# Keeping gate and up weights of the last two chunks' MLP in one set of buffers

## The chip, the cores and the metric

The kernel runs on one core of a Trainium2 chip. The metric is device time in microseconds (us) of one launch; lower is better.

## The reference

One transformer block is computed on a sequence of 2048 rows of width 640, in bfloat16. A vector `c` gives six modulation vectors.

```
mod = silu(c) @ w_mod                       # six vectors of 640: sa, ca, ga, sb, cb, gb
h = layernorm(x) * (1 + ca) + sa
q, k, v = h @ wqkv                          # 32 heads of 20
o = softmax(q @ k.T * 20**-0.5) @ v
x = x + ga * (o @ wo)
h = layernorm(x) * (1 + cb) + sb
x = x + gb * (((h @ w_gate) * (h @ w_up)) @ w_down)     # inner width 1536
```

## The kernel before

**Tiling.** The query rows are cut into five chunks (`CHUNKS`): three of 512 rows and two of 256. A chunk's attention is done in eight items of four heads each. Scores are made by TensorE (`L1491`) with keys on the partitions and queries along the free axis. Two ways lead from scores to exponentials. Most go to ScalarE, 1024 columns at a time (`L1529`, tile `PP`). The rest, in quads of four units of 512 columns, go to VectorE: it evicts each unit as int16 (`L1553`, tile `DB`), takes two terms out of the four with bit operations (`L1585` and `L1593`, tiles `DSS`), and multiplies one of them by the int16 bits read as bfloat16 (`L1590`, or in four pieces on GpSimd, `L1645`). TensorE multiplies both kinds by the values (`L2158`), summing an item in one PSUM bank. At the end of an item VectorE transposes that bank (`L1723`), takes the reciprocal of the sums (`L1727`), the product is made by GpSimd (`L1729`; for the last item by VectorE), VectorE transposes back (`L1737`, tile `OcT`), and four to five small DMAs copy the rows into place in `Ocp` (`L1750`).

**The suffix of a chunk.** When a chunk's eight items are done, `suffix(ci)` adds the work behind attention: the output projection (`wo` with `Ocp`, `L950` or `L946`), the residual and second layer norm, the transpose of the normed rows (`L1902`), gate and up blocks, the down projection (`wd` with `hprod`) and the stores (`L2048`). The gate and up weights are 12 blocks of 128 inner columns; each block is two loads of 160 KB (`L1956`), one for the gate and one for the up half. A block of a 256-row chunk is ten matmul steps into one PSUM bank; then the gate half is copied to `gsb` (`L1978` on VectorE, `L1979` on ScalarE) and multiplied with the up half into `hprod` (`L1985` on VectorE). For all chunks but the last, this work is laid between the score groups of the next chunk's attention, so chunk 3's MLP runs during chunk 4's attention; chunk 4's own suffix is the tail of the kernel. In chunk 3, TensorE's 128-wide operands are split into four 32-column matmuls ("quarters", `L950`), in chunk 4 they are whole (`L946`).

**Weight buffers.** Three buffers `stg` hold streamed blocks in rotation; a load waits until the block three before it has been used. The last chunk has, besides, ten resident buffers `stx` that are loaded ahead, without rotation. Five of them (`stx_121` to `stx_125`) lie in the storage of the queries `QT` of earlier chunks and may be loaded when those chunks' scores are done; five (`stx_130` to `stx_134`) lie in the storage of chunk 2's suffix and may be loaded when that suffix is finished. The number is computed from the space that is left:

```
nsx = min(11, (q_dead - t_size) // (2 * KD * 128 * 2))
...
while len(stx) < 11 and C.off + 2 * KD * 128 * 2 <= C.end:
    stx.append(C.alloc("stx", [128, 2, KD, 128], BF16))
nsq, nsx = nsx, len(stx)
```

**What sets the order.** The program is written down by a list scheduler (`Sched`) that runs while the kernel is built. Each piece of work is a task with an engine, an estimated duration, dependencies, a priority and a gate (a number of score groups that must have been reached). The result is a fixed order per engine, joined by semaphores. All loads and stores after the start are issued by one queue, SP's, in its order: a load that waits for its buffer holds up what stands behind it. The constants of the scheduler (`STAGE` and others) are the same in both kernels, but as durations and dependencies of tasks change, the order that it writes may change from there on.

Of the kernel before, what the change touches and what calls it, by code (L numbers as in the profile page):

```python
# [329 lines left out]
def emit_program(nc, sched, nsem_dma=56):  # L330
# [97 lines left out]
    with nc.Block() as block:  # L428
# [20 lines left out]
        def _(e):  # L449
# [4 lines left out]
CHUNKS = ((0, 512), (512, 512), (1024, 512), (1536, 256), (1792, 256))  # L454
# [3 lines left out]
         (1, 2, 1, 2, 2, 1, 1, 2),  # L458
         (0, 2, 1, 1, 3, 0, 3, 2))
HALF = (0, 0, 0, 0, 0)  # L460
D_LEAD = 0.451
NB0, NSS = 3, 3
XB0, XSS = 0, 0
# [130 lines left out]
def build_kernel(nc, A_x, A_wqkv, A_wo, B_x, B_w_gate, B_w_up, B_w_down, c, w_mod, out):  # L594
    S, D, H, DH = A_x.shape[1], A_x.shape[2], 32, 20
    KD = D // 128
# [3 lines left out]
    NSET = 8  # L600
    VW = DH + 1
    NC = len(CHUNKS)
# [127 lines left out]
    h2T = R2.alloc("h2T", [128, KD, 512], BF16)  # L730
# [22 lines left out]
    t_size = 0  # L753
    if NALT:
# [3 lines left out]
        t_size = T.off - qt_off  # L758
    nsx = min(11, (q_dead - t_size) // (2 * KD * 128 * 2))
    stx = [at("stx", [128, 2, KD, 128], BF16, qt_off + t_size + i * 2 * KD * 128 * 2) for i in range(nsx)]  # L760
    if NALT:
# [6 lines left out]
        nsq, nsx = nsx, len(stx)  # L768
# [44 lines left out]
    def act(dur, f, deps=(), prio=3.0, **k):  # L813
        return sc.add(Task("act", dur, f, deps, prio=prio, **k))

    def dma(eng, nbytes, f, deps=(), prio=3.0, **k):
        dur = k.pop("dur", 400.0)
        return sc.add(Task(eng, dur, f, deps, prio=prio, nbytes=nbytes, **k))
# [144 lines left out]
    def X(n):  # L963
        return max(n / 2.4 + 3.0, 60.0)
# [356 lines left out]
    for it, (ci, j) in enumerate(items):  # L1321
# [6 lines left out]
        for kg in range(nkg):  # L1328
            for s in range(4):
                u = Unit()  # L1330
# [18 lines left out]
    for it in range(len(items)):  # L1349
        na = len(item_info[it]["acts"])  # L1350
        dus = [u for q in item_info[it]["quads"] for u in q]
        for x, u in enumerate(dus):
            due.append(max(18.0, a0 + na * (x / len(dus) - STAGE.get(it, {}).get("DL", D_LEAD))))
        a0 += na
# [10 lines left out]
    NG = len(glist)  # L1365
# [10 lines left out]
    for tc in range(4):  # L1376
# [6 lines left out]
        if tc == 0:  # L1383
# [3 lines left out]
            x0_done = []  # L1387
        if tc == 3:
            x0_done = [t for l in t_xn.values() for t in l]
# [106 lines left out]
    score_q = []  # L1496
# [50 lines left out]
    for qi, (it, us) in enumerate(dquads):  # L1547
        st_ = d_state[qi]
        for x, u in enumerate(us):
            cell = {}  # L1550
# [219 lines left out]
    bset_done = [{}, {}]  # L1770
    sStg = [Slots(list(range(NSTG)), "stg") for _ in range(2)]

    def half_blocks(ci, nb, o_, t_h, h2T, hprod, hp, u_last, gate, pr, gb, bd):
        n = 256
        g_use = sfx_done.setdefault("gsb", {})
        for fc in range(nb):
# [38 lines left out]
                    sStg[w_].done(wbuf[w_]["i"], task)  # L1815
            r.last.on_start = off

    def suffix(ci):
        alt = NALT and ci >= NC - 2
        bd = bset_done[1 if NALT and ci == NC - 2 else 0]  # L1820
        hprod, h2T, xck, xn2 = set_r if not alt else set_t if ci == NC - 2 else set_c
# [6 lines left out]
        tail = ci == NC - 1  # L1828
        qf = full if tail and TAILX else quarters
        t0 = q0 // 128  # L1830
        gb = int(gstart[ci + 1]) if not tail else 0
# [18 lines left out]
        for tl in range(ntl):  # L1850
            ev = []
            for hf in range(2):
                mms = []
                for k in range(KD):
                    f = qf(320, lambda k=k, tl=tl: Ocp[:, slot, k, tl * 128:(tl + 1) * 128],
                                 lambda k=k, hf=hf: wo_sb[:, k, 320 * hf:320 * hf + 320], k == 0, k == KD - 1 and not tail)
# [8 lines left out]
                def after(r, tl=tl, hf=hf, fx=fx, pq=pq):  # L1865
                    f = lambda e: e.tensor_tensor(xck[:, tl, 320 * hf:320 * hf + 320], ps[:, r.b["b"], 0:320],
                                                  xck[:, tl, 320 * hf:320 * hf + 320], ALU.add)
                    if tail and OP_EARLY:
                        fs_ = fx if isinstance(fx, list) else [fx]
                        r.last = sc.add(Task("pe", C320, [lambda e, g_=g_: g_(e, r.b["b"]) for g_ in fs_], [r.last, oc_ready[ci][-1]],  # L1870
                                             ctr="pex", prio=pq - 1000, name=f"op{ci}.{tl}", mode=r.last.mode))
                    return [dve(ps_cost(320), f, [r.last, d_xc], prio=EV_OP if tail else 1)]
# [23 lines left out]
        tr_l = []  # L1896
        nhalf_ = HALF[ci] if n == 512 else 0

# [36 lines left out]
        hp = []  # L1935
# [9 lines left out]
            half_blocks(ci, nhalf_, o_, t_h2[5 * hf_:5 * hf_ + 5], h2T, hprod, hp, u_last, gate, pr, gb, bd)  # L1945
        g_use = sfx_done.setdefault("gsb", {})
        for fc in range(nhalf_, FT):
            use_x = tail and fc < nsx
            wbuf, dm = [], []
            for w_, wv in enumerate((wgv, wuv)):  # L1950
                cell = {}
                if use_x:
                    cell["t"] = stx[fc][:, w_, :, :]

                def f(e, wv=wv, fc=fc, cell=cell):
                    return e.dma_start(cell["t"], wv[:, :, fc * 128:(fc + 1) * 128])  # L1956
                t = dma("sp", 2 * 128 * KD * 128 * 2, f, sfx_done["qdead"] if use_x and fc < nsq else first if use_x else kp_use if ci == 0 else [], prio=16 + ci + .01 * fc,
                        gate=int(gstart[NC] - 40) if tail and not use_x else 0 if tail else max(0, gb + (STG_G0 if ci == 0 else STG_G)))
                if not use_x:
                    t.acq = [(sStg[w_], "s", 1)]  # L1960

                    def on0(task, cell=cell, w_=w_):
                        cell["i"] = task.slots["s"]
                        cell["t"] = stg[cell["i"]][:, w_, :, :]
                    t.on_start = on0
                wbuf.append(cell)
                dm.append(t)
            gs = fc % 2
            if n <= 256 and GU_ONE:
                mms = []  # L1970
                for w_ in range(2):
                    for k in range(KD):
                        f = qf(n, lambda k=k, cell=wbuf[w_]: cell["t"][:, k, :], lambda k=k: h2T[:, k, 0:n],
                                     k == 0, k == KD - 1, w_ * n)
                        mms.append((X(n), f))

                def after(r, gs=gs, fc=fc):
                    f = lambda e: e.tensor_copy(gsb[:, gs, 0:n], ps[:, r.b["b"], 0:n])  # L1978
                    fa = lambda e: e.copy(gsb[:, gs, 0:n], ps[:, r.b["b"], 0:n])  # L1979
                    ds = [r.last] + ([g_use[gs]] if gs in g_use else []) + sc_use  # L1980
                    if tail:
                        eg = act(n / 1.2 + 60, fa, ds, prio=1e6)
                    else:
                        eg = evac(n, ps_cost(n), f, fa, ds)
                    f = lambda e: e.tensor_tensor(hprod[:, fc, 0:n], ps[:, r.b["b"], n:2 * n], gsb[:, gs, 0:n], ALU.mult)  # L1985
                    return [eg, dve(ps_cost(n), f, [r.last, eg] + (first if alt else bd.get("hp", []) + proj_early + kv_last), prio=1)]
                r = Round(mms, t_h2 + dm + sfx_done.get("ul", []), after, pr(), gate=gate(2 * KD * n), name=f"u{ci}.{fc}")
                g_use[gs] = r.evac[1]
                hp.append(r.evac[1])
                u_last.append(r.last)  # L1990
                if not use_x:
                    def off(task, wbuf=wbuf):
                        for w_ in range(2):
                            sStg[w_].done(wbuf[w_]["i"], task)
                    r.last.on_start = off
                continue
            for w_ in range(2):
                mms = []
                for k in range(KD):
                    f = qf(n, lambda k=k, cell=wbuf[w_]: cell["t"][:, k, :], lambda k=k: h2T[:, k, 0:n],  # L2000
                                 k == 0, k == KD - 1)
                    mms.append((X(n), f))
                if w_ == 0:
                    def after(r, gs=gs):
                        f = lambda e: e.tensor_copy(gsb[:, gs, 0:n], ps[:, r.b["b"], 0:n])  # L2005
                        ds = [r.last] + ([g_use[gs]] if gs in g_use else []) + sc_use
                        fa = lambda e: e.copy(gsb[:, gs, 0:n], ps[:, r.b["b"], 0:n])
                        if tail:
                            return [act(n / 1.2 + 60, fa, ds, prio=1e6)]
                        return [evac(n, ps_cost(n), f, fa, ds)]  # L2010
                    r = Round(mms, t_h2 + [dm[0]] + sfx_done.get("ul", []), after, pr(), gate=gate(KD * n),
                              name=f"g{ci}.{fc}")
                    eg = r.evac[0]
                else:
                    def after(r, gs=gs, fc=fc, eg=eg):
                        f = lambda e: e.tensor_tensor(hprod[:, fc, 0:n], ps[:, r.b["b"], 0:n], gsb[:, gs, 0:n], ALU.mult)
                        return [dve(ps_cost(n), f, [r.last, eg] + (first if alt else bd.get("hp", []) + proj_early + kv_last), prio=1)]
                    r = Round(mms, t_h2 + [dm[1]] + sfx_done.get("ul", []), after, pr(), gate=gate(KD * n), name=f"u{ci}.{fc}")
                    g_use[gs] = r.evac[0]
                    hp.append(r.evac[0])  # L2020
                    u_last.append(r.last)
                if not use_x:
                    r.last.on_start = lambda task, w_=w_, cell=wbuf[w_]: sStg[w_].done(cell["i"], task)
        dn_last = []
        outs = []
        for tl in range(ntl):
# [4 lines left out]
            for (c_, w) in cuts:  # L2031
                mms = []
                for fc in range(FT):
                    f = qf(w, lambda fc=fc, tl=tl: hprod[:, fc, tl * 128:(tl + 1) * 128],
                           lambda fc=fc, c_=c_, w=w: wd_sb[:, fc, c_:c_ + w], fc == 0, fc == FT - 1)
# [6 lines left out]
                if tail and TAILX:  # L2042
# [6 lines left out]
                            prio=1))  # L2049
# [7 lines left out]
    for it in range(len(items)):  # L2057
        ci, j = items[it]
# [542 lines left out]
```

## Time and profile before

| | us |
|---|---|
| median of 3 runs | 813.44 (812.14 to 813.45) |
| the profiled execution | 813.98 |
| its span, first to last instruction | 812.1 |
| ScalarE's exponentials (`L1529`), 808 of them | 744.1 |
| TensorE's scores (`L1491`) | 316.2 |
| output projection of the last chunk starts | 778.61 |

Times within the trace count from the start of the span. A row of the timeline gives start, length, engine, line, operation, what is written and read, and how many instructions were merged; a bracket gives the idle time of that engine before it and what ended it. `PE` is TensorE, `PEld` its weight loads, `DVE` VectorE, `ACT` ScalarE, `POOL` GpSimd, and `SPq` the SP queue issuing a DMA. The granted clock of TensorE is a share of its full speed; its mean over the span is 0.998.

### The profile page before, as it was taken

The page shows a single profiled execution, that of the slowest core. Times are in us where ns is not written, and L with a number is a line of the kernel's source. Part 1 is how long each engine was busy: PE and PEld are TensorE (multiplying, and loading weights), DVE is VectorE, ACT ScalarE, POOL GpSimd, SP SyncE. Part 2 cuts the span into 40 slices and gives each one's busy share as a digit, 9 for nine tenths or more (in the row PEclk, how much of TensorE's full clock was granted, in tenths as well). Part 3 has the DMA queues.
Part 4 walks back from the last instruction along what each step waited for, and adds up shares of the span by engine and source line. Part 5 has one row for each costly group of instructions (what it writes and reads, how often), then busy time and mean ns, then how long its engine had stood idle before and what let it go on. Part 6 is the DMA issues. An engine that isn't in the chain of part 4 may idle for free.

```text
span 812.1 us, 29384 instructions
## 1 busy us (share of the span) xinstructions
PE 793.5 (98%) x12609; PEld 303.1 (37%) x12609; DVE 695.3 (86%) x1272; ACT 764.0 (94%) x853; POOL 324.2 (40%) x334
## 2 busy tenths in 40 slices
PE   8999999999999999999999999999999999999998
PEld 4433333222232232233333333332244334454567
DVE  7979987899989999989998999999698775788773
ACT  7889999999999999999999999999999999999722
POOL 3304266545453452264533434314565250534400
PEclk9999999999999999999999999999999999999999
DMA  9634211114330144100301221004001236005520
GB/s 311 204 85 105 71 46 38 49 38 122 89 67 25 36 126 112 34 6 25 102 5 30 51 57 31 15 19 91 13 6 37 48 79 150 17 21 131 116 70 17
DMA packets 116448, 54.74 MB, mean 67 GB/s; under 512 B 83915, under 2 KB 116319, under 8 KB 116319
## 3 DMA queue, kind: packets, MB, share of 16 engines
q1 hardware_dynamic: 115391, 51.72, 24.5%
q8 instruction: 100, 1.64, 0.8%
q10 hardware_dynamic: 928, 1.15, 0.4%
q14 instruction: 29, 0.24, 0.1%
HBM read 41.85 MB, written 8.41 MB: 62 GB/s over the span
## 4 chain that ended last, share of the span: by engine, by line
PE 64%; ACT 27%; DVE 3%; issue 3%; DMA 2%; SPq 1%; ACTq 0%
ACT PP L1529 27%; PE ps_all L1491 21%; PE ps_all L950 20%; PE ps_all L2158 15%; PE ps_all L946 3%; PE ps_all L1210 2%; DVE DB L1553 1%; PE ps_all L2525 1%; PE ps_all L1146 1%; DMA wm<-in_w_mod_dram 1%; SPq L1750 1%; PE ps_all L1902 1%; PE ps_all L1107 1%; DMA stg<-in_B_w_up_dram 0%; DVE DSS L1585 0%
## 5 line engine op out<-in xcount | busy, mean ns | idle before, releaser
L1529 ACT ACTIVATE PP<-ps_all 128x1024 bf16<-128x1024 f32 x808 | 744.1, 1134 | 10.3 <-PE ps_all L1491 6.2
L1645 POOL TENSOR_TENSOR DSS<-DB,DSS 128x512 bf16<-128x512 bf16 x228 | 259.2, 1155 | 337.8 <-DVE DSS L1593 257.6
L1553 DVE TENSOR_SCALAR DB<-ps_all 128x512 int16<-128x512 f32 x432 | 287.9, 682 | 58.6 <-PE ps_all L1491 56.3
L1491 PE MATMUL ps_all<-QT,KT 32*128 32x512 bf16 (+1 forms) x2560 | 316.2, 340 | 8.5 <-ACT PP L1529 6.6
L1491 PEld LDWEIGHTS ps_all<-QT,KT 32*128 32x128 bf16 x2560 | 82.2, 91 | 268.1 <-ACT PP L1529 233.4
L2158 PE MATMUL ps_all<-PP,Vf 128*32 128x512 bf16 (+1 forms) x2032 | 158.7, 344 | 0.1
L950 PE MATMUL ps_all<-h2T,stg 128*32 128x512 bf16 (+1 forms) x1776 | 117.8, 341 | 0.1
L2158 PE MATMUL ps_all<-DSS,Vf 128*32 128x512 bf16 (+2 forms) x1056 | 84.3, 346 | 1.1 <-DVE DSS L1590 1.1
L1585 DVE TENSOR_SCALAR DSS<-DB 128x2048 int16<-128x2048 int16 x108 | 74.8, 693 | 2.9 <-PE ps_all L2158 2.4
L1593 DVE TENSOR_SCALAR DSS<-DB 128x2048 int16<-128x2048 int16 x108 | 75.1, 696 | 1.9 <-PE ps_all L2158 1.9
L2158 PEld LDWEIGHTS ps_all<-PP,Vf 128*32 128x32 bf16 x2032 | 44.7, 94 | 81.5 <-issue 75.6
L1729 POOL TENSOR_TENSOR OTn<-OT,invT 128x512 bf16<-128x512 f32 (+1 forms) x39 | 37.1, 952 | 69.7 <-DVE invT L1727 69.6
L1590 DVE TENSOR_TENSOR DSS<-DB,DSS 128x2048 bf16<-128x2048 bf16 x51 | 63.2, 1239 | 0.0
L950 PE MATMUL ps_all<-wd,hprod 128*32 128x320 bf16 (+1 forms) x1328 | 60.7, 283 | 0.0
L950 PEld LDWEIGHTS ps_all<-h2T,stg 128*32 128x32 bf16 x1776 | 38.1, 95 | 31.3 <-issue 20.3
L950 PEld LDWEIGHTS ps_all<-wd,hprod 128*32 128x32 bf16 x1328 | 29.1, 96 | 19.5 <-issue 12.4
L2158 PEld LDWEIGHTS ps_all<-DSS,Vf 128*32 128x32 bf16 (+1 forms) x1056 | 26.5, 96 | 20.5 <-issue 10.7
L950 PE MATMUL ps_all<-wV,hT 128*32 128x320 bf16 (+1 forms) x700 | 32.5, 290 | 0.1
L1723 DVE STREAM_TRANSPOSE OT<-ps_all 128x512 f32<-128x512 f32 (+1 forms) x40 | 24.1, 602 | 9.6 <-PE ps_all L2158 9.5
L950 PE MATMUL ps_all<-wo,Ocp 128*32 128x320 bf16 (+1 forms) x668 | 30.5, 280 | 1.4 <-DMA Ocp<-OcT 0.6
L1210 PE MATMUL ps_all<-hT,wq 128*32 128x512 bf16 x375 | 31.3, 382 | 0.3 <-DVE DB L1553 0.2
L2005 DVE CAST gsb<-ps_all 128x512 bf16<-128x512 f32 x36 | 24.3, 676 | 5.4 <-PE ps_all L950 5.4
(126 smaller groups left out, 526.8 us busy)
## 6 DMA issues: line engine op xcount, KB each, us to landing
stg<-in_B_w_gate_dram SPq DMA_DIRECT2D x50, 160.0 KB
stg<-in_B_w_up_dram SPq DMA_DIRECT2D x50, 160.0 KB
QT<-q_rows SPq DMA_DIRECT2D x22, 128.0 KB
KT<-k_rows SPq DMA_DIRECT2D x84, 32.0 KB
wm<-in_w_mod_dram SPq DMA_DIRECT2D x3, 800.0 KB
x<-in_A_x_dram SPq DMA_DIRECT2D x7, 320.0 KB
xck<-in_A_x_dram SPq DMA_DIRECT2D x3, 640.0 KB
wd<-in_B_w_down_dram SPq DMA_DIRECT2D x1, 1920.0 KB
```

The costliest lines, as they stand in the source:

```text
L946: return lambda e, b: e.matmul(ps[:, b, c0:c0 + n], lhs(), rhs(), start=st, stop=sp)
L950: return lambda e, b: e.matmul(ps[32 * x:32 * x + 32, b, c0 + o:c0 + o + w], lhs()[:, 32 * x:32 * x + 32], rhs() if w == n else rhs()[:, o ...
L1210: f = [lambda e, b_, k=k, x=x: e.matmul(ps[x:x + min(32, w - x), b_, :], wx[:, k, r0 + x:r0 + min(x + 32, w)], hT[tc][:, k, :], tile_posit ...
L1491: ems.append(lambda e, i=i, kt=kt: e.matmul(dstf()[:, i * u.n:(i + 1) * u.n], KT[32 * u.s:32 * u.s + 32, u.j, kt * 128:(kt + 1) * 128], QT ...
L1529: return e.activation(PPs[g % 2][:, cellp["p"], 0:nu * 512], ps[:, b0:b0 + nu, :].rearrange("p b c -> p (b c)"), AFT.Exp, scale=ESCALE)
L1553: return e.tensor_scalar(DBl[st_["slot"]][:, x * 512:(x + 1) * 512], bank(cell["b"]), EBIAS, 0.0, op0=ALU.add, op1=ALU.max)
L1585: return e.tensor_scalar(DSl[st_["ss"][0]][:, :], DBl[st_["slot"]][:, :], 0x7F, 0x3F00, op0=ALU.bitwise_and, op1=ALU.bitwise_or)
L1590: return e.tensor_tensor(d, DBl[st_["slot"]][:, :].bitcast(BF16), d, ALU.mult)
L1593: return e.tensor_scalar(DSl[st_["ss"][1]][:, :], DBl[st_["slot"]][:, :], 0x7F80, 2, op0=ALU.bitwise_and, op1=ALU.bitwise_or)
L1645: return e.tensor_tensor(d, DBl[st_["slot"]][:, x * w:x * w + w].bitcast(BF16), d, ALU.mult)
L1729: f3 = lambda e: e.tensor_tensor(OTn[:, 0:n].rearrange("p (b c r) -> p b r c", c=32, r=2), OT[:, 0:n].rearrange("p (b r c) -> p b r c", c= ...
L2158: ems.append(lambda e, i=i, kt=kt, stt=stt, stp=stp: e.matmul(ps[32 * s:32 * s + mc, BPV, 0:u.n], Vf[:, (kt * H + 4 * u.j + s) * VW:(kt * ...
```

## The change

The next-to-last chunk's gate and up blocks no longer stream through `stg` as far as the last chunk has a resident buffer for the same block. They are loaded once, into `stx`, and both chunks read them there. The load is made by the next-to-last chunk's suffix; the last chunk takes over the buffer and the load's task (`resid`). The gate of these loads is 60 score groups before the start of the last chunk's scores. Each waits until its buffer's storage is dead: `stx_dead` gives the last score group of the earlier chunk in whose `QT` the buffer ends, and the other five wait for chunk 2's suffix as before. Blocks without a resident buffer stream as before, in both chunks.

```diff
+RESID, RES_G = 1, -60
...
+    resid = {}
+
+    def stx_dead(i):
+        hi = t_size + (i + 1) * 2 * KD * 128 * 2 - 1
+        off = 0
+        for z in range(NC):
+            off += NSET * CHUNKS[z][1] * 2
+            if hi < off:
+                break
+        return [score_q[g][0] for g in range(NG) if any(u.ci == z for u in score_q[g][1])][-1:] + x0_done
+
...
-            use_x = tail and fc < nsx
+            use_x = (tail or RESID and ci == NC - 2) and fc < nsx
...
+                if use_x and RESID:
+                    if not tail:
+                        b0_ = bset_done[0]
+                        resid[(fc, w_)] = dma("sp", 2 * 128 * KD * 128 * 2, f, stx_dead(fc) if fc < nsq else
+                                              b0_["tr"] + b0_["h2T"] + b0_["hp"] + b0_["out"], prio=16 + ci + .01 * fc,
+                                              gate=max(0, gb + RES_G))
+                    wbuf.append(cell)
+                    dm.append(resid[(fc, w_)])
+                    continue
```

Line numbers in the text are those of the kernel before; in the changed kernel `L1491` is `L1492`, `L1529` is `L1530`, `L950` is `L951` and `L2158` is `L2179`.

## The prediction

> **What bounds the kernel now.** I read the page first, then the granted clock and busy times by stage, then the chain that ended last, then each engine in order of time where the changed programs differ. The two programs' instruction orders, set side by side, are equal on every engine up to the first weight loads of this change; on TensorE they part only at the first gate block of the next-to-last chunk, at 740.88 us. So only what follows has to be costed, apart from the earlier loads.
>
> On the page TensorE and ScalarE look equally full.
>
> ```profile
> PE 793.5 (98%) x12609; PEld 303.1 (37%) x12609; DVE 695.3 (86%) x1272; ACT 764.0 (94%) x853; POOL 324.2 (40%) x334
> ```
>
> By stage they do not. Columns: stretch, length, busy time of PE, PEld, DVE, ACT, POOL, granted TensorE clock, DMA share, GB/s.
>
> ```profile
> 640.00:740.14 100.14, 100.03 (x2065) 44.68 (x2054) 71.14 (x132) 100.05 (x109) 34.58 (x37) 1.00 0.30 71
> 740.14:749.72 9.58, 9.57 (x244) 5.29 (x244) 7.80 (x17) 9.58 (x11) 3.92 (x4) 1.00 0.62 132
> 749.72:751.76 2.04, 0.07 (x3) 0.03 (x1) 1.81 (x4) 1.23 (x2) 0.58 (x1) 1.00 0.50 108
> 751.76:752.90 1.14, 1.14 (x32) 0.81 (x36) 0.00 (x0) 0.04 (x1) 0.00 (x0) 0.96 1.21 266
> 752.90:756.20 3.30, 3.30 (x54) 1.57 (x50) 1.82 (x4) 2.19 (x3) 1.73 (x2) 0.50 0.34 59
> 756.20:778.61 22.41, 20.89 (x575) 13.09 (x568) 19.72 (x39) 16.67 (x19) 8.54 (x9) 1.00 0.45 101
> 778.61:812.10 33.49, 30.85 (x410) 24.58 (x406) 15.94 (x43) 5.49 (x14) 1.10 (x2) 1.00 0.13 36
> ```
>
> Until 749.72 ScalarE never rests: the exponentials set the pace. Then TensorE stands for 2.04 us, runs 3.30 us at half clock, and from there to 778.61, where the output projection starts, TensorE is the bound and ScalarE idles. The chain names the wait (start, length, what):
>
> ```profile
> 744.66 1.06 SPq L1750
> ...
> 746.43 0.55 SPq L1750
> ...
> 747.11 0.51 SPq L1956
> ...
> 747.65 4.02 DMA stg<-in_B_w_up_dram
> ```
>
> The fourth gate/up pair goes into the ring buffer that the first block leaves at 742.98, but SP's queue reaches that load only at 747.11, behind ten loads for the last chunk (734.90 to 743.07) and five Ocp copies. TensorE in order of time, idle before in brackets:
>
> ```profile
> 749.39 0.40 PE L1491 MATMUL ps_all<-QT,KT 32*128 32x256 bf16 x6
> 751.76 0.73 PE L950 MATMUL ps_all<-h2Tt,stg 128*32 128x256 bf16 x24 [1.97 <-DMA stg<-in_B_w_up_dram]
> ...
> 768.63 0.29 PE L950 MATMUL ps_all<-h2Tt,stg 128*32 128x256 bf16 x4 [0.42 <-DVE hprodt L1985]
> ...
> 774.69 2.04 PE L950 MATMUL ps_all<-h2Tt,stg 128*32 128x256 bf16 x68
> 776.56 0.39 PE L2158 MATMUL ps_all<-PP,Vf 128*32 128x256 bf16 x8
> 778.01 0.63 PE L2158 MATMUL ps_all<-DSS,Vf 128*32 128x256 bf16 x16 [1.06 <-DVE DSS L1590]
> ```
>
> **What is removed.** The title says eleven blocks; the order has ten (stx_121 to 125 and 130 to 134), so 20 loads of 160 KB vanish and both chunks keep two streamed pairs. SP spent about 0.5 us per issue, but SP is never the last engine except at the wait above. That wait is 2.04 us. Its follower, the half clock, is 3.30 us at 0.50 and 1.14 us at 0.96, so about 1.7 us of clock. The span's mean clock is 0.998, and 812.1 x 0.002 is 1.6 us: this place holds all the clock that the run loses, so I count it to the wait.
>
> **TensorE's content by rows.** Unstalled, from one score start to the next at 747.63 to 748.51 is 0.88 us: 0.44 for the score run and the change of mode, the rest for twelve 256-column and eight 128-column matmuls, 0.0278 us and half that each. From 740.14 to 778.61 the old order has 31 score runs (13.64), 648 gate/up and value matmuls of 256 columns (18.01), 80 of 128 (1.11) and four fill matmuls (0.22): 32.98. Measured is 38.47. The 5.5 us difference is 2.04 wait, about 1.5 of half clock (rows there against the same rows elsewhere), 0.42 and 1.06 waits for VectorE, some 0.5 in pieces. The new order has 30 runs with mode change (13.20), three more score runs directly behind others (0.33 each, 0.99), 656 wide (18.24), 64 halves (0.89), the fill (0.22), and the first four down matmuls moved ahead of the output projection (0.14 by 4.53 us for 128): 33.68. With no wait at all the output projection would start at 740.14 + 33.68 = 773.82, 4.8 us earlier. That is the upper end of the gain.
>
> **Does ScalarE allow it?** It has 30 exponentials left from 740.69 at 0.933 us (11.19 for 12): it would end at 768.7. Walking both sums along the new order, TensorE's score starts stay within 0.3 us of ScalarE's pace up to the 25th group and fall behind after it. Nothing is lost to ScalarE, and gate/up work left behind the last scores (156 matmuls instead of 68) is only moved.
>
> **What is late next: VectorE.** I walked its new order from the same rows (score to evicted start 0.48; eviction 0.60, DSS term 0.60, product 1.13, gsb 0.33, hprod 0.37 back to back). From the eviction of group 17 (756.4) to the next-to-last eviction it has 8 evictions (4.80), 4 terms (2.40), 4 gsb (1.44), 4 hprod (1.48), a product (1.13), a transpose and reciprocal (0.50): 11.75 us, to be done by 768.6, when the last group's scores are there. That is 12.2 us. It fits, but bank releases then reach TensorE with only 0.05 to 0.2 us to spare, so I take 0.4 us of small waits, between none and the 1.5 us that arises if each row costs its printed 0.68 rather than 0.60.
>
> **The end of attention.** In the new order the OcT transpose of the next-to-last item stands behind the last evictions, ending near 769.4. In the old run OcT ended at 772.80 and the last of its five Ocp copies landed at 777.65: 4.85 us. So Ocp is there at 774.3. The last gate/up block ends near 773.3; ScalarE's copy (0.37) and hprod (0.42) with their signalling bring the first down matmul, which needs all twelve hprod, to 774.3 as well. Both are 0.5 us behind 773.82. Together: output projection at 773.82 + 0.5 + 0.4 = 774.7, gain 3.9 us. The last product chain (3.2 us from last scores in the old run, the 1.06 wait) now lies under 4.3 us of gate/up work.
>
> **The rest costs nothing, with its cover.** stx_121 to 124 now load from about 610 us, among chunk 2's weights: three issues ahead of four Ocp copies that wait for VectorE till 616.67 anyway, five around the stg reload of 621.73. That reload may land 3 us later than 624.16, but its block is first needed after 637; without that cover it would be 3 us. stx_130 to 134 keep their place and land by 746.75; the sixth block is needed about 757. Two loads for the last chunk's eleventh block go ahead of five Ocp copies at 743.11 (1.1 us later, needed at 774). The last pair comes after the final Ocp copies and is used near 800. After the output projection the order is the old one, 33.49 us less 0.14 for the four matmuls that already ran; the transpose behind the down matmuls has 0.25 us until xn2c would be late, so this hardly counts.
>
> The profiled execution took 813.98 (span 812.1 and 1.9 around it); 3.9 less is 810.1. The median of the runs is 0.5 below the profiled one, 813.44, so I forecast 809.6.
>
> [...] The row: TensorE idle 2.04 us, then half clock for 3.30 us. [...]
>
> **Rivals.** (a) Forecast, 0.60: 809.6, from 808.7 to 810.6. (b) VectorE becomes the bound, 0.18: for it speaks 11.75 us of work in 12.2; against it that the old run strung the same rows together at these intervals from 761 to 772. Printed durations make it 1.5 us late: 811.1. (c) The clock drop is not the wait's child and comes anyway, 0.05: the 1.5 us stay, 811.1. Against it: the mean of 0.998 leaves no other loss of clock in the run. (d) It does not do what it says for time, 0.08: the streamed wait reappears at stx_130 or elsewhere, 813.4; for it speaks only that one queue carries all loads, against it the ten-microsecond margins. (e) Slower, 0.09: the Ocp copies of the next-to-last item become the end. Their OcT stands behind two evictions and in front of them all of VectorE's saturated stretch. If it runs late by 4.4 us, the projection waits that long, the half clock follows (1.5 us) into a tail where TensorE is full, and 809.6 + 4.4 + 1.5 is 815.5. It decides from 4.0 us (4.0 + 1.5 is the gain of 3.9 and 1.6 more); VectorE would have to be a third slower than its rows.
>
> What this kernel's measurement can tell from no change is about 0.2%, 1.6 us: faster is below 811.8. (a), (b) and (c) are faster, 0.83; (d) is the same, 0.08; (e) slower, 0.09. The range is 808.6 (no waits, with the spread of the runs) to 812.3, leaving out (e) and most of (d).
>
> **What would show it.** Right: no row of TensorE that waits for a stg or stx load after 740; clock 1.00 throughout; the exponentials unbroken to about 763; the projection at 774 to 775.5; the tail after it 33.3 to 33.6 us; 40 stg loads each of gate and up weights against 50. Wrong: a clock below 1.00 near 753 without a wait (c); waits of TensorE for hprodt or DB that sum to over 1.5 us between 756 and 773 (b); the projection waiting for an Ocp landing (e); a tail longer than before.

## The result

The changed kernel takes 809.61 us (median of 5 runs, 809.32 to 809.66); the kernel before took 813.23 in the same rounds (811.98 to 813.45). The ratio is 0.9959, 95% interval 0.9945 to 0.9974. In a later set of rounds it was 809.80 (8 runs) against 811.96, 0.9969 (0.9958 to 0.9980). The changed kernel hardly moved between the two sets. The kernel before did, and the first experiment shows why.

The profiled execution took 809.65 us, its span 807.9. The columns of the first view are those of the table by stage in the prediction (stretch, length, busy time of PE, PEld, DVE, ACT, POOL, clock, DMA share, GB/s). Lines in the traces from here on are those of the changed kernel; besides those named above, `L946` is now `L947`, `L1585` `L1586`, `L1590` `L1591`, `L1593` `L1594`, `L1645` `L1646`, `L1956` `L1968` and `L1985` `L2006`.

```profile
740.14:749.72 9.58, 9.58 (x256) 5.49 (x252) 7.81 (x17) 9.58 (x12) 4.50 (x4) 1.00 0.69 132
749.72:756.20 6.48, 6.48 (x166) 3.46 (x160) 5.61 (x13) 6.48 (x8) 3.26 (x4) 1.00 0.02 4
756.20:774.50 18.30, 17.39 (x470) 11.58 (x471) 16.59 (x33) 13.45 (x17) 7.00 (x7) 1.00 0.04 9
774.50:807.90 33.40, 30.69 (x402) 24.59 (x402) 15.63 (x42) 5.48 (x14) 1.10 (x2) 1.00 0.10 30
```

Where the kernel before stood for 2.04 us and then ran at half clock, TensorE and ScalarE are now busy in all 6.48 us, at full clock. Almost no DMA runs there. The output projection starts at 774.50 instead of 778.61.

ScalarE, in order of time, shows the same: its exponentials run on without a gap to 763.47 (28.82 us from 734.65).

```profile
734.65 28.82 ACT L1530 ACTIVATE PP<-ps_all 128x1024 bf16<-128x1024 f32 x31
763.88 4.69 ACT L1530 ACTIVATE PP<-ps_all 128x1024 bf16<-128x1024 f32 x5 [0.41 <-PE ps_all L1492]
```

TensorE in front of the projection, idle time in brackets:

```profile
771.73 0.94 PE L951 MATMUL ps_all<-h2Tt,stg 128*32 128x256 bf16 x28
772.50 0.38 PE L2179 MATMUL ps_all<-PP,Vf 128*32 128x256 bf16 x4
773.46 0.63 PE L2179 MATMUL ps_all<-DSS,Vf 128*32 128x256 bf16 x16 [0.58 <-POOL DSS L1646]
773.91 0.32 PE L951 MATMUL ps_all<-wd,hprodt 128*32 128x320 bf16 x4
774.50 1.67 PE L947 MATMUL ps_all<-wo,Ocp 128*128 128x320 bf16 x11 [0.28 <-DMA Ocp<-OcT]
```

No row between 740 and the projection waits for a weight load. Two waits are left at the end: 0.58 us for a product on GpSimd and 0.28 for the last `Ocp` copy.

The page's total of bytes read:

```profile
HBM read 38.57 MB, written 8.41 MB: 58 GB/s over the span
```

It was 41.85 MB before; 20 loads of 160 KB are 3.28 MB. The page counts 40 loads into `stg` for each half instead of 50, as forecast.

**Where the 4.2 us of span went.** The stretch from the score run in front of the first gate block to the projection took 38.47 us (740.14 to 778.61) and takes 34.95 (739.55 to 774.50), a gain of 3.52. The tail went from 33.49 to 33.40. The other 0.59 us lie before 740 and are not the change's: that score run started at 740.14 in the execution shown before, but at 739.53 in another execution of the same kernel (experiment 1), and at 739.50 to 739.53 in experiments 2, 4 and 5, which keep the kernel before up to there.

### The profile page after: what moved, and what is told of

Its sections match the earlier page's. It is cut to its first block, busy times and chain, and to the rows that moved or that the text cites. A ratio compares the mean times of both kernels' runs of the same rounds, so it can differ in the third digit from the quotient of the medians.

```text
span 807.9 us, 29339 instructions
## 1 busy us (share of the span) xinstructions
PE 793.0 (98%) x12601; PEld 303.5 (38%) x12601; DVE 694.7 (86%) x1270; ACT 764.1 (95%) x855; POOL 324.3 (40%) x334
## 4 chain that ended last, share of the span: by engine, by line
PE 65%; ACT 30%; issue 3%; DVE 1%; SPq 0%; DMA 0%; POOL 0%; ACTq 0%; DVEq 0%; POOLq 0%
ACT PP L1530 30%; PE ps_all L1492 21%; PE ps_all L951 20%; PE ps_all L2179 14%; PE ps_all L947 3%; PE ps_all L1211 2%; PE ps_all L2544 1%; PE ps_all L2546 1%; PE ps_all L1147 1%; PE ps_all L1914 1%; PE ps_all L1108 1%; PE ps_all L972 0%; SPq L1751 0%; DMA Ocp<-OcT 0%; DVE DB L1554 0%
## 5 line engine op out<-in xcount | busy, mean ns | idle before, releaser
L1530 ACT ACTIVATE PP<-ps_all 128x1024 bf16<-128x1024 f32 x808 | 743.5, 1142 | 4.1 <-PE ps_all L1492 3.3
L1646 POOL TENSOR_TENSOR DSS<-DB,DSS 128x512 bf16<-128x512 bf16 x228 | 259.2, 1155 | 340.6 <-DVE DSS L1594 257.5
L1492 PE MATMUL ps_all<-QT,KT 32*128 32x512 bf16 (+1 forms) x2560 | 316.0, 340 | 8.8 <-ACT PP L1530 6.9
L1492 PEld LDWEIGHTS ps_all<-QT,KT 32*128 32x128 bf16 x2560 | 82.6, 91 | 268.4 <-ACT PP L1530 237.2
L2179 PE MATMUL ps_all<-PP,Vf 128*32 128x512 bf16 (+1 forms) x2032 | 159.0, 343 | 0.1
L951 PE MATMUL ps_all<-h2T,stg 128*32 128x512 bf16 (+1 forms) x1776 | 117.8, 341 | 0.1
L2179 PE MATMUL ps_all<-DSS,Vf 128*32 128x512 bf16 (+2 forms) x1056 | 84.0, 344 | 0.6 <-POOL DSS L1646 0.6
L1586 DVE TENSOR_SCALAR DSS<-DB 128x2048 int16<-128x2048 int16 x108 | 75.0, 695 | 2.9 <-PE ps_all L2179 2.4
L2179 PEld LDWEIGHTS ps_all<-PP,Vf 128*32 128x32 bf16 (+1 forms) x2032 | 44.8, 94 | 81.3 <-issue 75.4
L1594 DVE TENSOR_SCALAR DSS<-DB 128x2048 int16<-128x2048 int16 x108 | 75.3, 697 | 0.0
L1591 DVE TENSOR_TENSOR DSS<-DB,DSS 128x2048 bf16<-128x2048 bf16 x51 | 63.4, 1243 | 0.0
L951 PE MATMUL ps_all<-wd,hprod 128*32 128x320 bf16 (+1 forms) x1328 | 60.7, 283 | 0.0
L951 PEld LDWEIGHTS ps_all<-h2T,stg 128*32 128x32 bf16 x1776 | 38.1, 95 | 31.3 <-issue 20.6
L951 PEld LDWEIGHTS ps_all<-wd,hprod 128*32 128x32 bf16 x1328 | 29.1, 96 | 19.5 <-issue 12.4
L2179 PEld LDWEIGHTS ps_all<-DSS,Vf 128*32 128x32 bf16 (+1 forms) x1056 | 26.2, 95 | 20.2 <-issue 10.9
L951 PE MATMUL ps_all<-wV,hT 128*32 128x320 bf16 (+1 forms) x700 | 32.5, 290 | 0.1
L951 PE MATMUL ps_all<-wo,Ocp 128*32 128x320 bf16 (+1 forms) x668 | 30.5, 280 | 0.4 <-DVE DB L1554 0.3
```

The source lines that it names most:

```text
L951: return lambda e, b: e.matmul(ps[32 * x:32 * x + 32, b, c0 + o:c0 + o + w], lhs()[:, 32 * x:32 * x + 32], rhs() if w == n else rhs()[:, o ...
L1492: ems.append(lambda e, i=i, kt=kt: e.matmul(dstf()[:, i * u.n:(i + 1) * u.n], KT[32 * u.s:32 * u.s + 32, u.j, kt * 128:(kt + 1) * 128], QT ...
L1530: return e.activation(PPs[g % 2][:, cellp["p"], 0:nu * 512], ps[:, b0:b0 + nu, :].rearrange("p b c -> p (b c)"), AFT.Exp, scale=ESCALE)
L1586: return e.tensor_scalar(DSl[st_["ss"][0]][:, :], DBl[st_["slot"]][:, :], 0x7F, 0x3F00, op0=ALU.bitwise_and, op1=ALU.bitwise_or)
L1591: return e.tensor_tensor(d, DBl[st_["slot"]][:, :].bitcast(BF16), d, ALU.mult)
L1594: return e.tensor_scalar(DSl[st_["ss"][1]][:, :], DBl[st_["slot"]][:, :], 0x7F80, 2, op0=ALU.bitwise_and, op1=ALU.bitwise_or)
```

## The experiments

The experiments were run in three sets of rounds, each on another chip and each beside the kernel before, whose medians there were 812.90 (experiments 1 to 4), 811.74 (5, 6 and 9) and 811.96 us (7, 8 and the repeat of 9). Ratios are to the kernel before in the same rounds.

**1. The kernel before again.** No edit but empty lines, which bring the line numbers to those of the changed kernel (in experiments 2 to 5 too). The question is what makes its runs spread over 1.3 us.

> The kernel before, unchanged, five more times, to see the granted clock of every run beside its time. The runs of it so far fall in two groups, 811.98 and 812.14 against 813.23 to 813.45, 1.3 us apart, while those of the changed kernel lie within 0.34 us. Theory A (the half clock follows the 2.04 us wait in some executions only): runs with a mean clock of 1.000 at about 812.0 and runs with 0.998 at about 813.4, nothing between. Theory B (the half clock belongs to every execution, the spread is something else): 0.998 in all of them.

It took 813.0 us (12 runs, 810.5 to 814.68). This and the runs of the kernel before that accompany the later experiments make 88 executions with their mean clock:

| mean clock | executions | median us | lowest to highest |
|---|---|---|---|
| 1.000 | 50 | 811.6 | 810.2 to 812.9 |
| 0.997 or 0.998 | 29 | 813.2 | 812.8 to 814.6 |
| below 0.997 | 9 | 815.6 | 814.5 to 818.4 |

So the half clock is no fixed part of the kernel before. It comes in 38 of 88 executions, and one such stretch costs about 1.6 us. The two groups of theory A are there and meet at 812.8 to 812.9; a third, with a longer slow stretch or more than one, was not expected. The profiled execution is one of those. The group at 1.000 itself spans 2.7 us, which the theory doesn't explain either. The clock of the profiled execution by 3.40 us pieces (the view by stage, cut where the clock changes):

```profile
747.57:750.97 3.40, 1.62 (x48) 0.80 (x39) 2.55 (x5) 2.78 (x4) 2.13 (x2) 1.00 0.65 144
750.97:754.37 3.40, 3.28 (x53) 1.67 (x54) 0.69 (x1) 1.02 (x1) 0.08 (x1) 0.50 0.72 150
754.37:757.77 3.40, 3.40 (x57) 1.71 (x58) 1.14 (x3) 2.09 (x3) 3.13 (x4) 0.50 0.02 5
```

TensorE waits 1.90 us up to 751.09, and from 750.97 the clock is 0.50 for 6.80 us, twice 3.40.

**2. The wait filled with matmuls.** On the kernel before, TensorE gets 36 fill matmuls ahead of the first matmul that needs the late load; only that load's semaphore stays behind them.

```diff
+    late = [w for w in waits if any(w[0] is s for s in ld)]
...
+    fill = [lambda e, x=x: e.matmul(ps[32 * x:32 * x + 32, b, :]..., ident[:, 32 * x:32 * x + 32], idb, ...) for x in range(4)]
+    prog["pe"][k] = (late, t, inc)
+    prog["pe"].insert(k, ([w for w in waits if w not in late], Task("pe", 0.0, fill * 9), None))
```

> Nine sets of four fill matmuls (about 0.22 us a set, 1.97 us) are put on TensorE into the 1.97 us in which it waits for the streamed weights; their result is overwritten. The wait stays, TensorE is no longer idle in it. Theory A (the half clock is the wait's child): clock 1.000 in every run, no 3.3 us stretch at 0.50, time 812.0 within 0.3. Rival c of the prediction (the drop comes anyway): 0.998 and 813.4 as before. If the fills outlast the wait, up to 0.2 us more in both.

812.05 us (11 runs, 811.75 to 812.19), ratio 0.9992 (0.9983 to 1.0000), mean clock 1.000 in all eleven. TensorE in order of time, and then the two pieces by stage:

```profile
748.75 0.40 PE L1492 MATMUL ps_all<-QT,KT 32*128 32x256 bf16 x6
749.09 2.13 PE L2632 MATMUL ps_all<-ident 128*32 128x512 bf16 x36
751.09 0.73 PE L951 MATMUL ps_all<-h2Tt,stg 128*32 128x256 bf16 x24
```

```profile
749.20:752.60 3.40, 3.40 (x80) 1.76 (x75) 1.74 (x5) 1.52 (x3) 0.47 (x1) 1.00 0.82 179
752.60:756.00 3.40, 3.40 (x92) 1.99 (x92) 2.69 (x7) 3.40 (x5) 2.67 (x3) 1.00 0.03 7
```

The load is as late as it was, the DMA traffic is about the same (179 GB/s in the first of these stretches, 171 in the kernel before from 749.45 to 752.85), the order is the same, and the half clock is gone. Rival (c) of the prediction, that the drop comes anyway, falls. The wait itself is still there, only filled: 812.05 is 2.2 us above experiment 5, in which no load wait is left, and 2.4 above the changed kernel (both from other rounds). The eleven runs lie within 0.44 us, where those of the kernel before at full clock spread over 2.7. From these two spreads I estimate that part of the larger one is a wait that is longer in some executions than in others; no trace shows it.

**3. Ten loads put behind three streamed pairs.** On the kernel before, only SP's order is changed.

```diff
+    last = next(t for w, t, _ in sp if t.name == "L3.5.1")
...
+        if t.name[:2] == "L4" and 5 <= int(t.name.split(".")[1]) < 10:
+            out.append((w, Task("sp", 0.0, []), None))
+            kept.append(([], t, inc))
+            continue
+        out.append((w, t, inc))
+        if t is last:
+            out += kept
```

`L3.5.1` is the up half of chunk 3's sixth block. The empty task keeps the waits of a moved load where they were.

> The kernel before with all its loads; only SP's queue is changed: the ten loads of the last chunk's blocks 6 to 10 are issued behind the next-to-last chunk's loads for blocks 4, 5 and 6 instead of in front of them and of five Ocp copies. Every other engine's order is the old one. Theory A (what the change gains is the queue position of one streamed pair): no wait of TensorE for stg, clock 1.000, 2.04 us and the 1.5 us of half clock gone: 813.2 less 3.3 to 3.5 is 809.7 to 810.1. Rival (the gain comes from 20 loads and 3.3 MB fewer): the time of before, 813.2.

816.09 us (6 runs, 815.11 to 819.24), ratio 1.0049 (1.0033 to 1.0066): slower by 3.2 us, and neither theory's number. The chain of waits of its trace (start, length, what) says why:

```profile
759.43 0.54 SPq L1968
...
760.01 1.45 SPq L1968
...
761.50 4.45 DMA stg<-in_B_w_up_dram
765.95 0.09 issue
766.04 0.40 PE ps_all L951 x3
```

The wait at 750 is gone. The ten loads are now issued from 752.72 to 759.96, in front of the next reload of the ring, that of the seventh block. Its up half is issued at 761.50 and lands 4.45 us later, and TensorE stands for 4.52 us. The clock was below 1.000 in all six runs (0.994 to 0.996). I had only looked at the reload that was late before, not at the one that would stand behind the moved loads next. So the position of these ten loads on the queue alone moved the time 3.2 us up here (816.09 against 812.90), and 1.9 us down in experiment 5 (809.87 against 811.74).

The profiled execution, the slowest (819.24 us, clock 0.994), has a second slow stretch, far ahead of these loads: 3.40 us at 0.50 from 229.35. In the 3.40 us ahead of it TensorE had two short waits, 0.53 us for an exponential and 0.85 us for an `Ocp` copy, and was busy for 2.02 us.

**4. Two loads put behind.** The same edit for the last pair of the ten alone (`int(t.name.split(".")[1]) == 9`).

> As the kernel that moves ten loads, but only the last two of the ten (one pair) are put behind. The streamed pair is issued about 1.1 us earlier, so about 0.9 us of TensorE's wait is left. Theory A without a threshold (any such wait brings the half clock): 1.1 us gained in the runs with half clock, 812.1, clock still 0.998. Theory A with a threshold between 0.9 and 2 us: clock 1.000 and 1.1 + 1.4 us gained, 810.7 to 811.0.

810.15 us (12 runs, 809.74 to 813.17), ratio 0.9965 (0.9948 to 0.9981). Ten runs have clock 1.000, two 0.998 (812.38 and 813.17). The gain is larger than the 0.9 us of remaining wait allowed: the median of the ten, 810.1, is only 0.2 us above the 809.87 of experiment 5 (other rounds), in which no load wait is left. The profiled execution is one of the two with the drop, and in it TensorE still stands for 1.80 us: the up half was issued at 746.49 but landed 4.42 us later, 0.09 us before TensorE went on (the profile names a VectorE operation that ended in the same 0.1 us). How long the wait is in the other ten no trace shows, so the threshold that I looked for stays open here.

**5. Ten loads put behind everything.** The edit of experiment 3, with the ten loads in front of `L4.10.0`, the first load of the last chunk's eleventh block: behind all that chunk 3 still needs.

> The kernel before with all its loads; on SP's queue the ten loads of the last chunk's blocks 6 to 10 are issued behind everything that the next-to-last chunk still needs (its streamed pairs and all Ocp copies), at about 776 us; they are needed from about 790. Moving them behind blocks 4 to 6 only had put the wait before block 7 instead (4.52 us). Theory A (the gain is the queue position in front of a streamed reload, wherever it is): no wait of TensorE for a load after 740, clock 1.000 in every run, spread of a few tenths; row content 32.98 plus the old kernel's 1.5 us of VectorE waits and 0.5 of pieces, so the projection at about 775.1 and 809.9 to 810.4. Rival (the gain comes from 20 loads fewer): 812 to 813 with the old spread.

809.87 us (11 runs, 809.77 to 810.50), ratio 0.9979 (0.9970 to 0.9988), clock 1.000 in all eleven. The interval overlaps that of the changed kernel in its later rounds (0.9958 to 0.9980). It reads the same 41.85 MB as the kernel before, and every other engine has the old order. TensorE's only wait of note in front of the projection is the old one for VectorE:

```profile
773.90 0.63 PE L2179 MATMUL ps_all<-DSS,Vf 128*32 128x256 bf16 x16 [1.06 <-DVE DSS L1591]
774.50 1.79 PE L947 MATMUL ps_all<-wo,Ocp 128*128 128x320 bf16 x12
```

The projection starts at 774.50, as in the changed kernel. So the saving of 20 loads and 3.28 MB buys at most the 0.1 to 0.3 us between 809.87 and the changed kernel's 809.80 and 809.61, and the two were not run in the same rounds. What the change is worth is that no streamed reload stands behind ten loads that nobody needs yet.

**6. TensorE held still, with no load involved.** In the changed kernel TensorE waits, behind one group of scores, for three small ScalarE operations that follow that group's exponential.

```diff
+        for n in range(3):
+            if n:
+                q.wait_ge(sx, n)
+            r = q.activation(warm[:], mhalf[:, 0:1], AFT.Exp).then_inc(sx, 1)
...
+    act.insert(j + 1, ([(sems[e.ctr], e.val)], Task("act", 0.0, busy), None))
+    pe.insert(k + 1, ([(sx, 3)], Task("pe", 0.0, []), None))
```

> The changed kernel, with TensorE held still once near 749 us: behind one group of scores it waits for that group's exponential and three small ScalarE operations after it, about 2 us (1.2 for the exponential by the trace, some 0.25 each for the others). No load is touched. Theory A: the wait's length is added in every execution (811.4 to 811.9 with clock 1.000), and in about half of them, as in the kernel before, the half clock follows (0.998, about 1.4 us more, 813). Rival: the half clock needed the DMA traffic of that place, not the idle TensorE: clock 1.000 in all runs. [...]

812.8 us (11 runs, 811.14 to 815.74), 3.0 to 3.2 above the changed kernel in other rounds. Nine of eleven runs have a clock below 1.000, more than the half expected; the two at 1.000 took 811.14 and 813.10, and why the second is that slow no trace shows.

```profile
750.97 0.62 PE L951 MATMUL ps_all<-h2Tt,stx 128*32 128x256 bf16 x16 [1.82 <-ACT warm L2635]
```

```profile
749.20:752.60 3.40, 1.63 (x45) 0.99 (x48) 1.43 (x5) 2.27 (x6) 0.97 (x2) 1.00 0.00 0
752.60:756.00 3.40, 3.40 (x48) 1.30 (x48) 2.64 (x6) 2.43 (x3) 0.00 (x0) 0.50 0.02 5
```

An idle time of 1.82 us with no DMA traffic (0.00 share, 0 GB/s) was enough here for 3.40 us at half clock. With experiment 2 this shows both directions: with the idle time taken away and the late load left, the drop went (clock 1.000 in all eleven runs); with the idle time added without a load, it came (in nine of eleven).

**7. Half of the change.** Only blocks 6 to 10 are shared; the first five pairs of the next-to-last chunk stream as before.

```diff
-            use_x = (tail or RESID and ci == NC - 2) and fc < nsx
+            use_x = (tail or RESID and ci == NC - 2 and fc >= nsq) and fc < nsx
...
-                if use_x and RESID:
+                if use_x and RESID and fc >= nsq:
```

> Half of the change: only blocks 6 to 10 of the next-to-last chunk use the last chunk's loads; its first five pairs are streamed as before. Ten loads fewer than before, but the fourth pair again goes into the ring behind those ten loads and five Ocp copies. Theory A: TensorE waits near 750 for the stg load, 1.5 to 2.1 us, and some runs have a clock of 0.998; the order's planner, which sees no such wait, ends 1.4 us later than for the whole change, so 811.5 to 814, no gain over before. Rival (fewer loads): no wait, 809.6 to 811.

811.66 us (10 runs, 810.96 to 812.36), ratio 0.9995 (0.9985 to 1.0005), clock 1.000 in all ten. Right in the time, wrong in the way. The fourth block's load is as late as before (issued at 746.89, landed at 751.05), but TensorE doesn't wait for it: the scheduler put the sixth block, which is resident, in front of the fourth, and comes to the fourth at 753.24. Time is lost at the end instead, in another order of the last blocks, in which TensorE waits 0.98 us for VectorE:

```profile
774.35 1.00 PE L951 MATMUL ps_all<-wd,hprodt 128*32 128x320 bf16 x24 [0.98 <-DVE hprodt L2006]
775.18 0.61 PE L2179 MATMUL ps_all<-DSS,Vf 128*32 128x256 bf16 x16
775.61 2.89 PE L951 MATMUL ps_all<-wd,hprodt 128*32 128x320 bf16 x80
```

It doesn't tell the theories apart as I had meant. It does show that the late load (landed at 751.05) cost TensorE no wait here, where other work with its operands at hand was put in front until 753.24. Whether ten loads fewer are a gain it can't show, since the order changed with them; experiment 5 answers that.

**8. VectorE's room.** In the changed kernel two DSS terms of VectorE, near 758.6 and 764.6, are done twice. `f` is the instruction that makes the term.

```diff
+            f(e).then_inc(sx, 1)
+            e.wait_ge(sx, n + 1)
+            return f(e)
```

> The changed kernel with two of VectorE's 0.60 us terms (the DSS terms near 758.6 and 764.6) done twice, each time with the same result: 1.2 us and a little synchronisation more on VectorE in the stretch in which the prediction counted 11.75 us of rows in 12.2. By that count 0.45 us is spare and some of it already went into small waits: 0.8 to 1.2 us slower, 810.4 to 810.8. If VectorE were the bound already (rival b): 1.2 or more. If it has room: 809.6 to 809.8.

810.91 us (10 runs, 810.62 to 812.17), 1.1 above the changed kernel's 809.80 in the same rounds. The first doubled row of VectorE (the second, at 765.35, takes 1.41 us too), and the two new waits on TensorE (order of time):

```profile
758.62 1.41 DVE L1594 TENSOR_SCALAR DSS<-DB 128x2048 int16<-128x2048 int16 x2
```

```profile
760.50 0.40 PE L1492 MATMUL ps_all<-QT,KT 32*128 32x256 bf16 x6 [0.37 <-DVE hprodt L2006]
767.15 0.35 PE L951 MATMUL ps_all<-h2Tt,stx 128*32 128x256 bf16 x8 [0.62 <-DVE hprodt L2006]
```

A single one took 0.68 us, so VectorE got 2 x 0.73, 1.46 us more, and 1.1 of it reached the end. By this estimate VectorE had about 0.35 us to spare: rival (b) was near, but was not the case.

**9. Order constants chosen for the new order.** The change kept the constants. I tried other values for stages 37 to 39 and took two sets with which the scheduler's own estimate of the end came earliest. The first:

```diff
-XHALF = 1
+XHALF = 1; _T = {38: {'FILL_MIN': 3467.961, 'PVMIN': 3}, 39: {'D_LATE': 21, 'X_LATE': 6.641, 'HOLD': 116, 'PVCAP': 7, 'Z_LATE': 116.398, 'PVMAX': 3}, 37: {'EAGER': 5}}; STAGE.update({k: {**STAGE[k], **v} for k, v in _T.items()})
```

> The changed kernel, with the order constants of stages 37 to 39 chosen anew for it (the change kept those of the old order). The order's own planner ends 1.13 us earlier. If its ordering is right about what the chip does, the small DB waits and the last product's 0.58 us go: 808.4 to 809.2. If it only shifts work around, 809.6 (0.2 either way).

> As the other one with new order constants, from another choice of them (also one gate for streamed loads and one VectorE priority); the planner ends 1.20 us earlier. 808.4 to 809.2 if that holds on the chip, 809.6 if not.

808.54 us (4 runs, 808.42 to 808.80; ratio to the kernel before 0.9964, 0.9950 to 0.9977) and 808.68 (5 runs, 808.20 to 810.41; the slowest has a clock of 0.998, the other four 1.000). The first set and the changed kernel were then run in the same rounds:

> The changed kernel once more, on the chip and in the rounds of the following ones: theory A, 809.3 to 809.8 with clock 1.000 in every run, since no wait of 1.8 us or more is left in it.

> The first set of new order constants beside the changed kernel in the same rounds. It gave 808.42 to 808.80 before: 0.9 to 1.2 us below the changed kernel. If that was another chip's doing, 0.3 or less.

Changed kernel: 809.80 (8 runs, 809.25 to 810.37, all at clock 1.000; some runs are above the 809.8 I had set). New constants: 808.78 (6 runs, 808.44 to 810.35), ratio to the kernel before 0.9960 (0.9946 to 0.9974). Of the ten runs with this set of constants eight are below the lowest of the changed kernel's thirteen. TensorE in order of time, in front of the projection:

```profile
773.20 0.47 PE L2179 MATMUL ps_all<-DSS,Vf 128*32 128x256 bf16 x4
773.61 2.08 PE L947 MATMUL ps_all<-wo,Ocp 128*128 128x320 bf16 x14
```

Neither the wait for GpSimd's product nor the one for `Ocp` is there; the projection starts at 773.61. This version beats both kernels, by 1.0 us over the changed one.

## Why the prediction was right, and where it was not

**The wait.** Right. It was the one load behind ten others in SP's queue, not the number of loads: experiment 5 gets within 0.3 us of the changed kernel's time with all loads kept, and experiment 3 turns the same queue against the kernel.

**The half clock is the wait's child.** Right in kind (experiment 2, with the wait filled: clock 1.000 in eleven of eleven runs; experiment 6, with a wait put in: below 1.000 in nine of eleven). The term of the sum was mis-sized: I read the 1.5 us off one trace and took them as given, and they come in 38 of 88 executions. The gain against an execution without them is about 2 us (811.6 to 809.6), against one with them 3.6. The profiled execution had the drop, and by their times so had two of the three runs that I started from (813.45 and 813.44, not 812.14), so the forecast's starting point and its subtraction belonged together. The three times already had the two groups in them, and the prediction passed over that. That 809.6 was met to 0.01 us is luck: the stretch came out 0.39 us longer than forecast and began 0.59 us earlier for a reason outside the change, and the 0.5 us taken off between profiled execution and median did not recur (809.65 and 809.61). The slow stretches in the traces here last 3.40 or 6.80 us, and TensorE did work ahead of them: in the 3.40 us ahead of the drop it was busy for 1.43 us (the kernel before), 1.62 (experiment 1), 1.63 (experiment 6) and 2.02 (the early stretch of experiment 3). Under rival (c) the drop would have stayed with the wait gone; all thirteen runs of the changed kernel have a clock of 1.000.

**TensorE's content and the projection.** The stretch was forecast as 774.7 less 740.14, 34.56 us, and measured 34.95; the tail 33.35 and 33.40. The 33.68 of rows with 0.9 of waits became 33.68 with 1.27. What I had missed is GpSimd's last piece of the product before the last:

```profile
768.20 1.15 POOL L1646 TENSOR_TENSOR DSS<-DB,DSS 128x512 bf16<-128x512 bf16 x1
772.25 1.15 POOL L1646 TENSOR_TENSOR DSS<-DB,DSS 128x512 bf16<-128x512 bf16 x1 [2.90 <-DVE DSS L1591]
```

The prediction said that the last product chain lies under 4.3 us of gate/up work. VectorE's last product does. GpSimd, though, stood idle for 2.90 us until that product was done, and only then made its fourth piece of the product before it, which TensorE needed and which ended at 773.40. The piece reads nothing that VectorE's product writes: the wait is the scheduler's own, whose `lock` makes a GpSimd piece depend on the VectorE operation of this kind that was placed shortly ahead of it. The `Ocp` copies were also slower: the last two took 3.16 and 2.60 us from issue to landing where the row used had 1.83, and landed at 774.45. Without GpSimd's wait the copies would still have held the projection to 774.45; with copies as fast as the row used it would have started 0.28 us earlier. So the two steps ("So Ocp is there at 774.3" and "now lies under 4.3 us of gate/up work") together put the projection 0.4 us too early.

**VectorE.** Right: the rows fitted, with small waits; experiment 8 finds 0.35 us of room against 0.45 counted. The count itself is uneven: four `gsb` at the 0.33 us given are 1.32, not 1.44, which makes 11.63 us and 0.57 of room.

**ScalarE and the early loads.** Right: no gap up to 763, and no wait for a weight load from 600 to 740 either. (The "eleven blocks" of the prediction are the upper limit `min(11, ...)` in the code; ten are shared.)

**Rivals (d) and (e).** The streamed wait did not return in the changed kernel. But experiment 3 is rival (d)'s mechanism with rival (e)'s price: a reload behind ten loads at another place, 4.52 us, and a slow stretch of 6.8 us (765.25 to 772.08).

## What to carry to other kernels

Before crediting a change with the bytes that it saves, ask which transfer was late and what stood ahead of it on its issue queue; reordering that queue may give the same time, and moving loads back must be followed to the next transfer that will stand behind them. A wait of TensorE of about 2 us (2.04 in the profiled execution) cost here nearly twice its length where the half clock followed (about 1.6 us more), and that was in some executions only (38 of 88): when run times fall in two groups, read the mean clock of each run before sizing anything from a single trace. After such a change, retune what was tuned for the old order: here that gave another 1.0 us.

## What the runs showed of the hardware

- Half clock after an idle time of 1.8 to 2.0 us (the kernel before, experiments 1, 4 and 6), and once after two short waits of together 1.4 us (experiment 3, at 229 us). The slow stretch is 3.40 us or twice that. In the four traces with one idle time of 1.8 to 2.0 us, that idle time lies, to about 0.15 us, within the 3.40 us ahead of the slow stretch. Why only some executions of the kernel before have the slow stretch (38 of 88) is not shown: no run here controlled where the wait falls or how long it is.
- The clock came back after 3.40 us in which TensorE was busy throughout (the kernel before, experiments 4 and 6, both stretches of experiment 3). In experiment 1 it did not come back after 3.40 us with 3.28 of work.
- The issue-to-landing time of one 160 KB load varied from 2.6 to 5.8 us between 740 and 780 us in the trace of experiment 3. The longest (5.5 to 5.8) were the last three of the ten loads and the gate half of the reload behind them; the up half, for which TensorE waited, took 4.45.
